# Chunk attention and two feed-forward layers on one Trainium2 core: the weights' preparation moved and split, and the last first product of a pair placed inside the first second product

## The chip, the core and the metric

One core of one Trainium2 chip runs one program. The time is device microseconds (us) of an execution; three executions of the kernel before took 1644.35 to 1645.06 us, median 1645.0. A profiled execution gives the rows below; their times count from the start of its span.

## The reference

```
scores = scale * q_c @ k_c^T            # chunks of 64 rows, 8 batches, 8 heads, 576 rows, 64 columns
attn   = exp(scores - max) / (sum + 1e-9)
x      = attn @ v_c                     # as 4608 tokens x 512
h = x @ w_in;  g = s * relu(h)**2 + b;        y   = g @ w_out     # 512 -> 2048 -> 512
h = y @ w_in2; g = h * sigmoid(1.702 * h);    out = g @ w_out2    # 512 -> 2048 -> 512
```

All is float32; the weights come as 64-bit floats that the kernel turns into float32 itself.

## The kernel before

**Numbers.** Every float32 operand of a large product is kept as two tiles, hi (rounded by ScalarE) and lo (VectorE's difference), and a product is three matmuls: lo by hi, hi by hi, hi by lo. A matmul has 128 rows of weights and 512 columns.

**Blocks.** The 4608 tokens are nine blocks of 512. Seven blocks of the first layer and one of the second are computed plainly: `gemm_in` (L554, 12 matmuls into one of two banks h) for each of 16 slices of the inner dimension, relu and square on ScalarE (L566, L567), hi and lo (L102, L103), and `gemm_out` (L629, 12 matmuls into four banks acc). A bank h is free again when its relu has read it.

**Pairs.** The other ten passes are taken as five pairs of blocks, by a scheme with seven products instead of eight, M1 to M7, on halves and their sums and differences. `PAIRS` lists them as layer and first block: (1, 1), (0, 7), (1, 3), (1, 5), (1, 7), layer 0 being the first. In each, eight steps i make the seven first products (`first`, L735): M1, M6, M7 and M4 add into one bank x of step i, M5 and M3 into a bank d, M2 has a bank b. `quarter` (L754 to L761) turns the banks into the four quarters of g: 11 from b, 12 from d, 22 from x after M7, 21 from x after M4. Then the seven second products follow (`second`, L834), each over the same eight i and for two halves z of its output; the first of them is M1. The banks of the second products for z = 0 and z = 1 are those that held x of steps 6 and 7, tags acc2 and acc3.

**Weights.** The first layer's weights are decoded at the start and stay as hi and lo. Beside the blocks run sixteen pieces of work for the pairs, one for each i of eight and each of w_in and w_out:
- `decode_second` loads two tiles of the second layer's weights (512 KB each), decodes them (L124 to L130 on ScalarE, VectorE and GpSimd), stores them in DRAM (`w2_dram`, by GpSimd's queue), makes four sums of their quarters on GpSimd (`add_quarters`, L221 to L224), rounds them on ScalarE (L209, 128x1024), subtracts (L211), and stores hi and lo.
- `sums` does the same with the first layer's weights, from the kept hi and lo (L240), with two roundings (L247) and four stores.
- `copies` copies three quarters of kept hi and lo to DRAM (256 KB each, L263).

When the first layer's plain blocks end, `second_weights` brings the 32 decoded tiles back (L228, 256 KB each) and splits them again (L150, L151).

**Order.** Each call has a time on a plan (`at`, `steps_at`); 32 units are one plain block. The calls are emitted in the order of these times, and a scheduler with a model of the engines then sets the order on each engine. Each engine takes its instructions strictly in that order. `behind` adds an order between two instructions of an engine. Loads and stores go through SP's queue in order, but for GpSimd's and a few of ScalarE's. Three buffers hold what is loaded for decoding (wst), ten hold temporary tiles (tmp), four hold v and the sums (vs).

Of the kernel before, what the change touches and what calls it, by code (L numbers as in the profile page):

```python
# [6 lines left out]
F32 = mybir.dt.float32  # L7
# [28 lines left out]

PLACE = {"M1": 0, "M2": 1, "M4": 2, "M5": 3, "M6": 4, "M7": 5, "M3": 6}
BANK = {"M1": "x", "M6": "x", "M7": "x", "M4": "x", "M5": "d", "M3": "d", "M2": "b"}  # L40
PAIRS = ((1, 1), (0, 7), (1, 3), (1, 5), (1, 7))
OUT_ORDER = ("M1", "M5", "M6", "M2", "M7", "M3", "M4")
# [3 lines left out]
def chunk_attention_two_ffn(ctx, tc, q, k, v, w1_in, w1_out, s, b, w2_in, w2_out, out):  # L46
# [145 lines left out]
    def decode_second(kind, i):  # L192
        tiles = i, i + KF // 2
        sts, ms = [], []
        for t in tiles:
            sts.append(staged())
            load_f64[kind](w2_in if kind == "wi" else w2_out, t, sts[-1])
            yield
        for t, st in zip(tiles, sts):
            m, c = tmp("wm"), tmp("wc")  # L200
            for _ in decode(st, m, c):
                pass
            nc.gpsimd.dma_start(out=w2_dram[kind][t], in_=m)
            ms.append(m.rearrange("p (t c) -> p t c", c=2 * P))
            yield
        s, hi = (st.rearrange("p f z -> p (f z)").bitcast(F32).rearrange("p (t c) -> p t c", c=2 * P) for st in sts)
        add_quarters(kind, s, ms)
        yield
        nc.scalar.activation(out=hi.bitcast(F32R), in_=s, func=AF.Copy)  # L209
        yield  # L210
        nc.vector.tensor_tensor(out=s.bitcast(F32R), in0=s, in1=hi, op=ALU.subtract)  # L211
        for part, src in enumerate((hi, s)):
            nc.sync.dma_start(out=sums_to(1, kind, i)[:, 3:7, part].rearrange("p m k c -> p m (k c)"), in_=src)

    def add_quarters(kind, s, tiles):

        one, two = tiles
        a11, a22 = one[:, 0, :], two[:, 1, :]
        a12, a21 = (one[:, 1, :], two[:, 0, :]) if kind == "wi" else (two[:, 0, :], one[:, 1, :])
        s1, s2, s3, s4 = (s[:, t, :] for t in range(4))  # L220
        nc.gpsimd.tensor_tensor(out=s1, in0=a21, in1=a22, op=ALU.add)  # L221
        nc.gpsimd.tensor_tensor(out=s3, in0=a11, in1=a21, op=ALU.subtract)
        nc.gpsimd.tensor_tensor(out=s2, in0=s1, in1=a11, op=ALU.subtract)
        nc.gpsimd.tensor_tensor(out=s4, in0=a12, in1=s2, op=ALU.subtract)  # L224

    def second_weights(kind, i):
        m = tmp("wm")
        nc.sync.dma_start(out=m, in_=w2_dram[kind][i])  # L228
        W[1, kind, i] = resident(1, kind, i, m)

    def sums_to(f, kind, i):
# [2 lines left out]
    def sums(kind, i):  # L234

        q = []
        for t in (i, i + KF // 2):
            hi, lo = (kept_parts[0, kind, t][:, a, :] for a in range(2))
            q.append(apool.tile([P, NB_MAX], F32, tag="vs", name="vs", bufs=HP))
            nc.vector.tensor_tensor(out=q[-1], in0=hi, in1=lo, op=ALU.add)  # L240
        yield
        q = [t.rearrange("p (t c) -> p t c", c=2 * P) for t in q]
        s = staged().rearrange("p f z -> p (f z)").bitcast(F32).rearrange("p (t c) -> p t c", c=2 * P)
        add_quarters(kind, s, q)
        yield
        for n, hi in enumerate(q):
            nc.scalar.activation(out=hi.bitcast(F32R), in_=s[:, 2 * n:2 * n + 2, :], func=AF.Copy)  # L247
        yield
        to = sums_to(0, kind, i)
        for n, hi in enumerate(q):  # L250
            part = s[:, 2 * n:2 * n + 2, :]
            nc.vector.tensor_tensor(out=part.bitcast(F32R), in0=part, in1=hi, op=ALU.subtract)
            for a, src in enumerate((hi, part)):
                nc.sync.dma_start(
                    out=to[:, 3 + 2 * n:5 + 2 * n, a].rearrange("p m k c -> p m (k c)"), in_=src
                )

    def copies(f, kind, i):

# [401 lines left out]
    class Halves:  # L661
# [63 lines left out]
        def first(self, i, m):  # L725
            key = i, BANK[m]
            start = key not in self.ps
            if start:
                self.bank(key, BANK[m], f"acc{i % KD}")
            w = self.wi[i][PLACE[m]]  # L730
            for k in range(HK):
                xh, xl = self.x[m, k]
                hi, lo = w[:, k, 0, :], w[:, k, 1, :]
                for a, (l_, r_) in enumerate(((lo, xh), (hi, xh), (hi, xl))):
                    nc.tensor.matmul(  # L735
                        out=self.ps[key], lhsT=l_, rhs=r_,
                        start=start and k == 0 and a == 0, stop=k == HK - 1 and a == 2,
                        skip_group_check=not start,
                    )

        def keep(self, key, name):
            self.kept[key[0], name] = t = tmp("kept")
# [25 lines left out]
        def plan_first(self):  # L768
            self.wi = {}

            def load(i):
                self.w = {}
                self.load_wi(i)
                self.wi[i] = self.w
            for i in range(HF):
                t = self.base + 3.5 * i
                at(t - 9, load, i)
                at(t, self.rooms_g, i)

                for n, m in ((0, "M1"), (0.5, "M5"), (1.5, "M6"), (2, "M2"), (2.5, "M3"), (3, "M7"), (4.5, "M4")):  # L780
                    at(t + n, self.first, i, m)
                at(t + 0.6, self.keep, (i, "x"), "M1")
                at(t + 1.1, self.keep, (i, "d"), "M5")
                at(t + 2.1, self.keep, (i, "x"), "M16")
                at(t + 2.6, self.quarter, i, "11")
                at(t + 3.1, self.quarter, i, "12")
                at(t + 3.6, self.quarter, i, "22")
                at(t + 5.1, self.quarter, i, "21")
# [33 lines left out]

        def second(self, n, i, zs=(0, 1)):
            m = OUT_ORDER[n]
            hi, lo = self.op[n, i]
            w = self.wo[n, i // 2]
            for z in zs:
                key = "out", z, BANK[m]
                start = m in ("M1", "M5", "M2")
                if start and i == 0:  # L830
                    self.bank(key, BANK[m], f"acc{HK + z}")
                wh, wl = (w[:, i % 2, z, part, :] for part in range(2))
                for a, (l_, r_) in enumerate(((wl, hi), (wh, hi), (wh, lo))):
                    nc.tensor.matmul(  # L834
                        out=self.ps[key], lhsT=l_, rhs=r_,
                        start=start and i == 0 and a == 0, stop=i == HF - 1 and a == 2,
                        skip_group_check=not start,
                    )

        def keep_out(self, z, bank, name):  # L840
            self.kept[z, name] = t = tmp("kept")
# [27 lines left out]
        def plan_second(self):  # L869
            self.wo = {}  # L870
            base = self.base + 3.5 * HF
            for n, m in enumerate(OUT_ORDER):
                for r in range(HF // 2):
                    at(base + 4 * n + r - 9, self.load_wo, n, r)
                for i in range(HF):
                    t = base + 4 * n + 0.5 * i
                    at(t - 3, self.operand, n, i)
                    if not (self.last and m == "M4"):
                        at(t, self.second, n, i)
                done = base + 4 * n + 4.1  # L880
                if self.last and m == "M4":
                    for z in range(2):
                        for i in range(HF):
                            at(base + 4 * n + 2 * z + 0.25 * i, self.second, n, i, (z,))
                        at(base + 4 * n + 2 * z + 2.1, self.result, "21", z)
                    continue
                for z in range(2):
                    if m in ("M1", "M5", "M6"):
                        at(done, self.keep_out, z, BANK[m], {"M6": "M16"}.get(m, m))
                    else:  # L890
                        at(done, self.result, {"M2": "11", "M7": "22", "M3": "12", "M4": "21"}[m], z)
# [67 lines left out]
        plan_attention(j)  # L959
    plan_y(0)  # L960
    for n, (i, kind) in enumerate((i, kind) for i in range(KF // 2) for kind in ("wi", "wo")):
        t = 56 + 9.3 * n
        steps_at([(t + d, 1) for d in (0, 1, 2.5, 4, 6, 8.5, 9.7)], lambda kind=kind, i=i: decode_second(kind, i))
        steps_at([(t + d, 1) for d in (2.2, 2.5, 5, 6.2)], lambda kind=kind, i=i: sums(kind, i))
        at(t + 3, copies, 0, kind, i)
    for i in range(KF):
        for n, kind in enumerate(("wi", "wo")):
            t = NS * (SINGLE - 1) + 2 * i + 1 + 3 * n
            at(t, second_weights, kind, i)
            if i >= KF // 2:  # L970
                at(t + 3, copies, 1, kind, i - KF // 2)
    def first_product(*a):
        G[a] = gemm_in(*a)

# [40 lines left out]
```

## Time and profile before

| | |
|---|---|
| three executions | 1644.35 to 1645.06 us, median 1645.0 |
| the profiled execution | 1644.05 us |
| its span, first to last instruction | 1642.3 us, mean granted TensorE clock 0.989 |
| busy: PE, DVE, ACT, POOL | 1584.4, 1125.5, 823.4, 250.7 us |

PE is TensorE, PEld its weight loads, DVE VectorE, ACT ScalarE, POOL GpSimd, SP SyncE (SPq its queue of transfers). PE is busy for 96% of the span, so what is left to gain is nearly all in the 58 us in which it is not, and in the stretches at the lower clock.

### The profile page before, as it was taken

What the parts mean: (1) busy time and instruction counts of PE and PEld (TensorE: products, weight loads), DVE (VectorE), ACT (ScalarE), POOL (GpSimd) and SP (SyncE); (2) the same over time, 40 slices, a digit from 0 to 9 for tenths busy, and PEclk for the clock granted to TensorE, in tenths of its full rate; (3) what the DMA queues carried; (4) which work ended last, traced back from release to release, by engine and by line L of the source; (5) the groups of instructions that cost most, each with busy time, mean ns of one, the idle gap of its engine ahead of it and who ended that gap; (6) DMA issues with size and microseconds to landing.
All of it is one profiled execution on the core that took longest, in us unless ns stands there. A gap on an engine that the chain in (4) does not pass through costs nothing.

```text
span 1642.3 us, 24873 instructions
## 1 busy us (share of the span) xinstructions
PE 1584.4 (96%) x8840; PEld 1295.1 (79%) x8840; DVE 1125.5 (69%) x1836; ACT 823.4 (50%) x1427; POOL 250.7 (15%) x286
## 2 busy tenths in 40 slices
PE   6889999999999999999999999999999999999998
PEld 4768887778888888777888788888887888788876
DVE  5667667768776676766745696369368946984685
ACT  3766424445544545545334564776345535543552
POOL 1344214234333334200000000000001000100000
PEclk8899999999999999999999999999999999999999
DMA  9747667666665666899606777786668686777764
GB/s 232 224 159 205 201 171 220 169 178 174 187 170 158 171 193 164 243 278 289 203 27 187 235 224 192 213 274 205 196 193 265 179 225 210 249 192 214 218 194 76
DMA packets 392396, 326.74 MB, mean 199 GB/s; under 512 B 256592, under 2 KB 330320, under 8 KB 392272
## 3 DMA queue, kind: packets, MB, share of 16 engines
q1 hardware_dynamic: 382096, 301.81, 65.0%
q0 software_dynamic: 5760, 18.88, 3.4%
q10 hardware_dynamic: 4416, 4.46, 0.8%
q8 instruction: 70, 1.15, 0.3%
q14 instruction: 54, 0.44, 0.1%
HBM read 232.78 MB, written 92.27 MB: 198 GB/s over the span
## 4 chain that ended last, share of the span: by engine, by line
PE 78%; DVE 7%; DMA 5%; ACT 3%; SPq 2%; issue 2%; POOL 2%; DVEq 0%; POOLq 0%; ACTq 0%
PE acc L629 15%; PE h L554 14%; PE x L735 13%; PE x L834 13%; PE d L834 7%; PE d L735 7%; PE b L735 3%; PE b L834 3%; DMA wm<-w_wi 2%; DVE pt L320 1%; PE xT L330 1%; PE sc L351 1%; SPq L452 1%; SPq L294 1%; DVE gl L103 1%
## 5 line engine op out<-in xcount | busy, mean ns | idle before, releaser
L554 PE MATMUL h<-xh,wi 128*128 128x512 f32 x1024 | 326.1, 400 | 19.1 <-ACT r L566 9.5
L629 PE MATMUL acc<-gh,wo 128*128 128x512 f32 x896 | 277.1, 393 | 2.7 <-ACT gh L102 2.7
L554 PEld LDWEIGHTS h<-xh,wi 128*128 128x128 f32 x1024 | 193.0, 192 | 62.6 <-ACT r L566 11.5
L554 PE MATMUL h<-xl,wi 128*128 128x512 f32 x512 | 202.2, 396 | 0.0
L629 PEld LDWEIGHTS acc<-gh,wo 128*128 128x128 f32 x896 | 166.3, 188 | 38.7 <-ACT gh L102 3.6
L629 PE MATMUL acc<-gl,wo 128*128 128x512 f32 x448 | 172.7, 392 | 2.0 <-DVE gl L103 1.9
L811 ACT ACTIVATE op<-wo 128x512 fp32r<-128x512 f32 x160 | 99.7, 631 | 98.1 <-PE x L834 35.9
L834 PE MATMUL x<-op,wi 128*128 128x512 f32 x540 | 130.7, 389 | 0.0
L735 PE MATMUL x<-xh,wi 128*128 128x512 f32 x400 | 124.3, 391 | 3.1 <-DVE wo L754 3.1
L812 DVE TENSOR_TENSOR op<-wo,op 128x512 fp32r<-128x512 f32 x160 | 107.2, 683 | 17.4 <-ACT op L811 15.9
L834 PEld LDWEIGHTS x<-op,wi 128*128 128x128 f32 x540 | 101.4, 188 | 21.1
L554 PEld LDWEIGHTS h<-xl,wi 128*128 128x128 f32 x512 | 98.3, 192 | 21.1
L659 DVE TENSOR_TENSOR wo<-wo 128x512 f32<-128x512 f32 x160 | 107.4, 686 | 4.5 <-ACT wo L757 3.7
L761 DVE TENSOR_TENSOR wo<-wo,r 128x512 f32<-128x512 f32 x96 | 66.0, 691 | 63.8 <-ACT r L760 63.4
L128 POOL TENSOR_TENSOR wm<-wm,wc 128x512 int32<-128x512 int32 x52 | 73.4, 1414 | 216.0 <-DVE wm L127 111.9
L674 POOL DMA_DIRECT2D xr<-y x32 | 17.6, 549 | 564.5 <-DVE op L812 278.8
L629 PEld LDWEIGHTS acc<-gl,wo 128*128 128x128 f32 x448 | 83.9, 188 | 21.6 <-DVE gl L103 4.0
L320 DVE STREAM_TRANSPOSE pt<-p 32x256 f32<-32x256 f32 x224 | 97.7, 436 | 3.9
L760 ACT ACTIVATE r<-wo 128x512 f32<-128x512 f32 x96 | 60.7, 632 | 75.8 <-DVE wo L754 75.1
L811 ACT ACTIVATE gh<-wo 128x512 fp32r<-128x512 f32 x120 | 74.7, 631 | 47.4 <-PE x L834 13.6
L812 DVE TENSOR_TENSOR gl<-wo,gh 128x512 fp32r<-128x512 f32 x120 | 81.4, 687 | 18.5 <-ACT gh L811 14.3
L735 PEld LDWEIGHTS x<-xh,wi 128*128 128x128 f32 x400 | 74.7, 188 | 20.5 <-DVE wo L754 5.2
(162 smaller groups left out, 3028.6 us busy)
## 6 DMA issues: line engine op xcount, KB each, us to landing
wi<-wo_sums SPq DMA_DIRECT2D x140, 512.0 KB, 4.2
wi<-wi_sums SPq DMA_DIRECT2D x120, 512.0 KB, 4.0
wst<-in_moe_w_out SPq DMA_DIRECT2D x32, 512.0 KB, 4.2
wst<-in_moe_w_in SPq DMA_DIRECT2D x24, 512.0 KB, 4.5
wi_sums<-wi SPq DMA_DIRECT2D x48, 256.0 KB, 4.0
wo_sums<-wo SPq DMA_DIRECT2D x48, 256.0 KB, 4.1
wi<-wi_sums SPq DMA_DIRECT2D x40, 256.0 KB, 3.6
y<-ost SPq DMA_DIRECT2D x36, 256.0 KB, 3.7
```

The source lines that it names most:

```text
L128: nc.gpsimd.tensor_tensor(out=t, in0=t, in1=c.bitcast(I32), op=ALU.add)
L320: nc.vector.transpose(out=pt[r.start + ek * BK:r.start + (ek + 1) * BK, :, eq * BK:(eq + 1) * BK], in_=p[r.start + eq * BK:r.start + (eq + ...
L554: nc.tensor.matmul(out=ps, lhsT=w_[:, kk, :], rhs=x_, start=kk == 0 and a == 0, stop=kk == KD - 1 and a == 2,)
L629: nc.tensor.matmul(out=acc[m], lhsT=l_, rhs=r_, start=i == 0 and a == 0, stop=i == KF - 1 and a == 2)
L659: nc.vector.tensor_tensor(out=to, in0=one, in1=two, op=ALU.subtract)
L674: nc.gpsimd.dma_start(out=t, in_=(y_dram if self.f else x_dram)[self.j + c][:, k + a * HK, :])
L735: nc.tensor.matmul(out=self.ps[key], lhsT=l_, rhs=r_, start=start and k == 0 and a == 0, stop=k == HK - 1 and a == 2, skip_group_check=not ...
L760: nc.scalar.activation(out=r, in_=h, func=AF.Sigmoid, scale=1.702)
L761: nc.vector.tensor_tensor(out=g, in0=h, in1=r, op=ALU.mult)
L811: nc.scalar.activation(out=hi, in_=src, func=AF.Copy)
L812: nc.vector.tensor_tensor(out=lo, in0=src, in1=hi.bitcast(F32), op=ALU.subtract)
L834: nc.tensor.matmul(out=self.ps[key], lhsT=l_, rhs=r_, start=start and i == 0 and a == 0, stop=i == HF - 1 and a == 2, skip_group_check=not ...
```

## The change

- The sixteen pieces start 6 units later, and within a piece the rounding of the decoded weights' sums and what follows comes 1 unit later; so does the rounding in `sums`.
- `sums` makes its four sums in place, in the two tiles vs that held the operands; the buffer wst is then taken only for the rounded halves. `PLACE` gives the products another order in DRAM (M1, M2, M4, M6, M7, M3, M5), which suits the tiles as they now lie.
- `second_weights` is split: the load three units before its old time, the splitting at the old time. The copies of the second weights get times of their own, after the last plain block of the first layer by the plan.
- In each pair M4 of the last step is planned at 4.2 instead of 4.5, the first second product goes z by z for six of its eight i, and its matmuls from i = 3 on are ordered behind that M4.

```diff
-PLACE = {"M1": 0, "M2": 1, "M4": 2, "M5": 3, "M6": 4, "M7": 5, "M3": 6}
+PLACE = {"M1": 0, "M2": 1, "M4": 2, "M6": 3, "M7": 4, "M3": 5, "M5": 6}
...
-        add_quarters(kind, s, ms)
+        add_quarters(kind, ms, [s[:, t, :] for t in (3, 0, 1, 2)])
...
-    def add_quarters(kind, s, tiles):
+    def add_quarters(kind, tiles, to=None):
...
-        s1, s2, s3, s4 = (s[:, t, :] for t in range(4))
+        s1, s2, s3, s4 = to or (a22, a11, a21, a12)
...
         nc.sync.dma_start(out=m, in_=w2_dram[kind][i])
+        yield
         W[1, kind, i] = resident(1, kind, i, m)
...
-        s = staged().rearrange("p f z -> p (f z)").bitcast(F32).rearrange("p (t c) -> p t c", c=2 * P)
-        add_quarters(kind, s, q)
+        add_quarters(kind, q)
         yield
-        for n, hi in enumerate(q):
-            nc.scalar.activation(out=hi.bitcast(F32R), in_=s[:, 2 * n:2 * n + 2, :], func=AF.Copy)
+        his = staged().rearrange("p f z -> p (f z)").bitcast(F32).rearrange("p (t c) -> p t c", c=2 * P)
+        his = [his[:, 2 * n:2 * n + 2, :] for n in range(2)]
+        for src, hi in zip(q, his):
+            nc.scalar.activation(out=hi.bitcast(F32R), in_=src, func=AF.Copy)
...
+            if m == "M4" and i == HF - 1:
+                marks["last first product", self.f, self.j] = latest(mybir.EngineType.PE)
...
-                for n, m in ((0, "M1"), (0.5, "M5"), (1.5, "M6"), (2, "M2"), (2.5, "M3"), (3, "M7"), (4.5, "M4")):
+                for n, m in ((0, "M1"), (0.5, "M5"), (1.5, "M6"), (2, "M2"), (2.5, "M3"), (3, "M7"), (4.2 if i == HF - 1 else 4.5, "M4")):
...
+            old = len(nc.cur_bb.bb.instructions)
...
+            if n == 0 and i == 3:
+                behind(old, mybir.EngineType.PE, ("last first product", self.f, self.j))
...
-                    if not (self.last and m == "M4"):
+                    if n == 0 and i < 6:
+                        for z in range(2):
+                            at(base + 6 / 4 * z + 0.25 * i, self.second, n, i, (z,))
+                    elif not (self.last and m == "M4"):
                         at(t, self.second, n, i)
...
-        t = 56 + 9.3 * n
-        steps_at([(t + d, 1) for d in (0, 1, 2.5, 4, 6, 8.5, 9.7)], lambda kind=kind, i=i: decode_second(kind, i))
-        steps_at([(t + d, 1) for d in (2.2, 2.5, 5, 6.2)], lambda kind=kind, i=i: sums(kind, i))
+        t = 62 + 9.3 * n
+        steps_at([(t + d, 1) for d in (0, 1, 2.5, 4, 6, 9.5, 10.7)], lambda kind=kind, i=i: decode_second(kind, i))
+        steps_at([(t + d, 1) for d in (2.2, 2.5, 6, 7.2)], lambda kind=kind, i=i: sums(kind, i))
...
-            at(t, second_weights, kind, i)
+            steps_at(((t - 3, 1), (t, 1)), lambda kind=kind, i=i: second_weights(kind, i))
             if i >= KF // 2:
-                at(t + 3, copies, 1, kind, i - KF // 2)
+                at(NS * SINGLE + 2.5 * (i - KF // 2) + 2 + n, copies, 1, kind, i - KF // 2)
```

In the listings that follow, a row is line, operation, written tile, read tiles, shape and count.

PE, at the end of the first products of the first pair. x_9405 is the bank x of step 7 (its last four rows here are M4), x_9499 the bank of the first second product for z = 0, x_9503 (after: x_9552) that for z = 1. Before:

```order
L834 MATMUL x_9499<-gh_9449,wi_9309 128x512 x2
L834 MATMUL x_9499<-gl_9450,wi_9309 128x512
L834 MATMUL x_9499<-op_9465,wi_9309 128x512 x3
L834 MATMUL x_9499<-op_9476,wi_9335 128x512 x3
L834 MATMUL x_9499<-op_9491,wi_9335 128x512 x3
L834 MATMUL x_9499<-op_9507,wi_9356 128x512 x3
L735 MATMUL x_9405<-xh_8477,wi_9214 128x512 x2
L735 MATMUL x_9405<-xl_8478,wi_9214 128x512
L735 MATMUL x_9405<-xo_8741,wi_9214 128x512 x2
L735 MATMUL x_9405<-xo_8742,wi_9214 128x512
L834 MATMUL x_9503<-gh_9423,wi_9289 128x512 x2
L834 MATMUL x_9503<-gl_9424,wi_9289 128x512
```

The same place after:

```order
L837 MATMUL x_9499<-gl_9438,wi_9289 128x512
L837 MATMUL x_9499<-gh_9449,wi_9309 128x512 x2
L837 MATMUL x_9499<-gl_9450,wi_9309 128x512
L735 MATMUL x_9405<-xh_8471,wi_9214 128x512 x2
L735 MATMUL x_9405<-xl_8472,wi_9214 128x512
L735 MATMUL x_9405<-xo_8741,wi_9214 128x512 x2
L735 MATMUL x_9405<-xo_8742,wi_9214 128x512
L837 MATMUL x_9499<-op_9465,wi_9309 128x512 x3
L837 MATMUL x_9499<-op_9476,wi_9335 128x512 x3
L837 MATMUL x_9499<-op_9491,wi_9335 128x512 x3
L837 MATMUL x_9499<-op_9503,wi_9356 128x512 x3
L837 MATMUL x_9552<-gh_9423,wi_9289 128x512 x2
```

M4 of step 7 has moved up past twelve matmuls of z = 0, which now stand between it and the first matmul of z = 1. All five pairs have this.

ACT, in the first piece whose rounding L209 stands close before a relu (L566) of block 2. wst_2790 and wst_2799 (after: wst_2677 and wst_2698) are the two buffers of the decoded weights, h the banks of `gemm_in`. Before:

```order
L247 ACTIVATE vs_2821<-wst_2833 128x512
L247 ACTIVATE vs_2823<-wst_2833 128x512
L102 ACTIVATE xh_2921<-xT_2879 128x512
L209 ACTIVATE wst_2799<-wst_2790 128x1024
L364 ACTIVATE p_2943<-p_2943 128x512
L566 ACTIVATE r_2982<-h_2967 128x512
L566 ACTIVATE r_3024<-h_3009 128x512
```

The corresponding place after, one piece earlier in the row of pieces (the first w_in piece instead of the first w_out piece):

```order
L249 ACTIVATE wst_2804<-vs_2731 128x512
L102 ACTIVATE xh_2885<-xT_2845 128x512
L249 ACTIVATE wst_2804<-vs_2729 128x512
L209 ACTIVATE wst_2698<-wst_2677 128x1024
L364 ACTIVATE p_2907<-p_2907 128x512
L566 ACTIVATE r_2944<-h_2929 128x512
L567 ACTIVATE r_2944<-r_2944 128x512
L566 ACTIVATE r_2981<-h_2966 128x512
```

One whole piece, which before stood here already done, has moved behind this block's start; the two roundings of `sums` (L247, now L249) and L209 still stand ahead of the relu.

SP, around the load of w2_wo1 (the second w_out tile brought back) in block 6. Before:

```order
L228 DMA wm_7038<-w2_wi2_102 128x512
L254 DMA wo_sums0_148<-wst_7093 128x2x256
L294 DMA ks_7251<-in_k 32x14x32
L339 DMA x7_150<-xo_7043 128x512
L294 DMA ks_7251<-in_k 32x14x32 x2
L294 DMA qs_7250<-in_q 32x2x32 x4
L294 DMA ks_7251<-in_k 32x2x32 x4
L304 DMA vs_7370<-in_v 64x7x64 x2
L304 DMA vs_7370<-in_v 64x64
L228 DMA wm_7098<-w2_wo1_117 128x512
L228 DMA wm_7131<-w2_wi3_103 128x512
L228 DMA wm_7156<-w2_wo2_118 128x512
```

After:

```order
L228 DMA wm_6866<-w2_wi2_102 128x512
L263 DMA wi_sums10_140<-wi_6840 128x2x256 x2
L294 DMA qs_7216<-in_q 32x14x32 x4
L228 DMA wm_6907<-w2_wo1_117 128x512
L294 DMA ks_7217<-in_k 32x14x32 x4
L650 DMA y5_157<-ost_6924 128x512
L294 DMA qs_7216<-in_q 32x2x32
L650 DMA y5_157<-ost_6930 128x512
L650 DMA y5_157<-ost_6927 128x512
L294 DMA qs_7216<-in_q 32x2x32
L534 DMA yst_6936<-y0_152 128x512
L228 DMA wm_6941<-w2_wi3_103 128x512
```

The load of w2_wo1 now stands before the loads of k and before this block's stores of y, where it stood behind them and behind v; the copies (L263) still stand among the loads.

## Rows read from the trace of the kernel before

**Rows 1.** The page: span, and busy us by engine.

```profile
span 1642.3 us, 24873 instructions
PE 1584.4 (96%) x8840; PEld 1295.1 (79%) x8840; DVE 1125.5 (69%) x1836; ACT 823.4 (50%) x1427; POOL 250.7 (15%) x286
```

**Rows 2.** PE's waits, whole span: waiter, releaser: us in total, times, longest.

```profile
PE h L554 <- ACT r L566: 9.5, 4, 4.3
...
PE x L834 <- DVE wo L761: 5.8, 4, 1.5
...
PE acc L629 <- ACT gh L102: 2.7, 1, 2.7
...
PE x L834 <- ACT wo L756: 0.7, 1, 0.7
```

**Rows 3.** Stretches: us, busy of PE, PEld, DVE, ACT, POOL, clock, DMA, GB/s.

```profile
240.00:280.00 40.00, 38.01 (x264) 30.10 (x263) 29.00 (x44) 16.24 (x28) 15.98 (x18) 0.96 0.80 223
280.00:320.00 40.00, 35.67 (x201) 28.48 (x200) 35.16 (x53) 18.22 (x31) 12.64 (x14) 0.96 0.69 178
...
720.00:760.00 40.00, 37.17 (x212) 29.02 (x211) 24.61 (x42) 23.56 (x41) 0.00 (x0) 1.00 1.03 300
```

**Rows 4.** Timeline, end of a pair's first products: start, us, instruction, idle before.

```profile
1245.72 0.69 DVE L754 TENSOR_TENSOR wo<-x,kept 128x512 f32<-128x512 f32 x1 [0.23 <-PE x L735]
...
1247.56 2.88 PE L834 MATMUL x<-op,wi 128*128 128x512 f32 x12
...
1251.90 0.60 ACT L760 ACTIVATE r<-x 128x512 f32<-128x512 f32 x1 [1.41 <-PE x L735]
1252.53 0.69 DVE L761 TENSOR_TENSOR wo<-x,r 128x512 f32<-128x512 f32 x1 [1.32 <-ACT r L760]
...
1253.27 0.73 PE L834 MATMUL x<-gh,wi 128*128 128x512 f32 x2 [1.47 <-DVE wo L761]
```

**Rows 5.** Timeline of all engines, block 2, around PE's longest wait there.

```profile
286.66 1.05 POOL L224 TENSOR_TENSOR wst<-wm,wst 128x256 f32<-128x256 f32 x1
...
287.74 1.06 ACT L209 ACTIVATE wst<-wst 128x1024 fp32r<-128x1024 f32 x1 [3.94 <-POOL wst L224]
...
290.76 1.06 ACT L566 ACTIVATE r<-h 128x512 f32<-128x512 f32 x2
...
291.39 1.22 PE L554 MATMUL h<-xh,wi 128*128 128x512 f32 x2 [4.33 <-ACT r L566]
```

**Rows 6.** POOL's timeline, the start of the run that ends in rows 5.

```profile
273.75 1.52 POOL L128 TENSOR_TENSOR wm<-wm,wc 128x512 int32<-128x512 int32 x1 [10.90 <-DVE wm L127]
```

**Rows 7.** Groups of instructions by line: busy, mean ns of one.

```profile
L812 DVE TENSOR_TENSOR gl<-wo,gh 128x512 fp32r<-128x512 f32 x120 | 81.4, 687 | 18.5 <-ACT gh L811 14.3 <-PE x L834 2.2 <-PE b L834 0.7
...
L128 POOL TENSOR_TENSOR wm<-wm,wc 128x512 int32<-128x512 int32 x52 | 73.4, 1414 | 216.0 <-DVE wm L127 111.9 <-ACT r L567 22.2 <-ACT gh L102 22.0
L103 DVE TENSOR_TENSOR gl<-r,gh 128x512 fp32r<-128x512 f32 x80 | 69.5, 873 | 8.2 <-ACT gh L102 7.9
```

**Rows 8.** Timeline, block 6: a second weight is loaded, split, and waited for.

```profile
683.99 0.53 SPq L228 DMA_DIRECT2D wm<-w_wo  x1
...
687.04 0.63 ACT L150 ACTIVATE wo<-wm 128x512 fp32r<-128x512 f32 x1 [4.87 <-DMA wm<-w_wo]
687.58 0.61 ACT L102 ACTIVATE gh<-r 128x512 fp32r<-128x512 f32 x1
...
688.25 0.73 PE L629 MATMUL acc<-gh,wo 128*128 128x512 f32 x2 [2.67 <-ACT gh L102]
```

**Rows 9.** PE's timeline, 720 to 800 us: two of its waits.

```profile
732.19 0.73 PE L554 MATMUL h<-xh,wi 128*128 128x512 f32 x2 [2.26 <-ACT r L566]
...
770.96 0.73 PE L554 MATMUL h<-xh,wi 128*128 128x512 f32 x2 [1.47 <-DVE r L570]
```

**Rows 10.** Transfers: count, KB each, median us from issue to landing.

```profile
wm<-w_wo SPq DMA_DIRECT2D x16, 256.0 KB, 4.5
```

**Rows 11.** DVE's timeline, 276 to 285 us.

```profile
278.97 4.23 DVE L103 TENSOR_TENSOR gl<-r,gh 128x512 fp32r<-128x512 f32 x1
```

More of the change, by code (lines that the diff above doesn't have):

```diff
@@ L242, in sums @@
         q = [t.rearrange("p (t c) -> p t c", c=2 * P) for t in q]
-        s = staged().rearrange("p f z -> p (f z)").bitcast(F32).rearrange("p (t c) -> p t c", c=2 * P)
-        add_quarters(kind, s, q)
+        add_quarters(kind, q)
         yield
-        for n, hi in enumerate(q):
-            nc.scalar.activation(out=hi.bitcast(F32R), in_=s[:, 2 * n:2 * n + 2, :], func=AF.Copy)
+        his = staged().rearrange("p f z -> p (f z)").bitcast(F32).rearrange("p (t c) -> p t c", c=2 * P)
+        his = [his[:, 2 * n:2 * n + 2, :] for n in range(2)]
+        for src, hi in zip(q, his):
+            nc.scalar.activation(out=hi.bitcast(F32R), in_=src, func=AF.Copy)
         yield
[L249 to L256, printed above, removed]
+        sums = sums_to(0, kind, i)[:, 3:7]
+        for n, (src, hi) in enumerate(zip(q, his)):
+            nc.vector.tensor_tensor(out=src.bitcast(F32R), in0=src, in1=hi, op=ALU.subtract)
+            to = sums[:, n::2] if kind == "wi" else sums[:, 2 * n:2 * n + 2]
+            for a, part in enumerate((hi, src)):
+                nc.sync.dma_start(out=to[:, :, a].rearrange("p m k c -> p m (k c)"), in_=part)
     def copies(f, kind, i):
```

## The prediction

> **What bounds the kernel now.** I read the busy times first: PE is busy 1584.4 of 1642.3 us [rows 1], so the time can fall only where PE stands still (58 us) or runs at the lower clock. Second, PE's waits with their releasers over the whole span. Those that the change can touch are five [rows 2]: 9.5 us for relu L566 on ScalarE in four waits, 5.8 us in four for the quarter L761, 0.7 us in one for L756 (the same place in the pair of layer 0), 2.7 us in one for the rounding L102. A good part of the other idle time lies at the start, before the first pieces, where the order on PE is the same before and after. Third, the table of stretches: in 240 to 320 us PE is busy 73.68 of 80 us and the granted clock is 0.96 in both stretches of 40 us; in 720 to 760 us PE is busy 37.17 of 40 us and the transfers use all that the 16 DMA engines have, share 1.03 [rows 3]. Last, the timeline at each of these waits [rows 4, 5, 8, 9], to see who is late and why. So there are three places with something to gain: the end of each pair's first products, block 2 with the first pieces, and block 6 with the second weights.
>
> **Part 1, the pairs.** Before, M4 of step 7 is the last thing that PE issues ahead of the first matmul for z = 1, which writes the very bank that M4 filled. ScalarE (L760, 0.60 us) and VectorE (L761, 0.69 us) must read that bank first, so PE stands for 1.47 us [rows 4]. After, twelve matmuls of z = 0 stand between M4 and z = 1. They are those that took 2.88 us as one row [rows 4], which covers the 1.47 us twice over. Does M4 get a wait in exchange? It adds to bank x of step 7 after the quarter L754 has read it. L754 ended at 1245.72 + 0.69 = 1246.41 us, and M4 can now start where the twelve began, at 1247.56 us: 1.15 us to spare. The operands of the twelve matmuls were there earlier than they are now needed. On ScalarE and VectorE L760 and L761 come right behind what they followed before, so they start 2.88 us earlier too. All five pairs have the same order here: the gain is 5.8 + 0.7 = 6.5 us [rows 2]. If the cover failed in part, it would be worth less, but hardly below 5. The new times of the second product's z halves alter nothing else: the matmuls are the same. The new order of loading (M5 last) costs nothing as long as each step's weights come two steps ahead, as they do in the order.
>
> **Part 2, the pieces in blocks 2 to 5.** The pieces' work is the same in count and size: the sums in place are the same four operations of VectorE's size on GpSimd, with the same roundings and stores. What changes is what stands in front of whom. Before, L209 stood on ScalarE just ahead of a relu while GpSimd was still at the sums: it waited 3.94 us for L224, ScalarE's queue stood with it, and PE waited 4.33 us for the relu behind it [rows 5]. GpSimd's run for this piece began at 273.75 us [rows 6] and ended at 286.66 + 1.05 = 287.71 us. After, a piece stands here whose L209 still comes ahead of the relu, but whose decoding started earlier relative to the block. By hand I follow it: two L128 of 1.41 us [rows 7], eight sums of about 1.05 us [rows 5], 11.2 us in all, from about 271.5 (estimate, 2 us ahead of rows 6 because its decoding isn't behind the first two transposes) to 282.7 us, or to 284.8 us with gaps like those of before (13.96 us in rows 5 and 6 for the like work). L209 takes 1.06 us, and 2 us later the relu can run, at 284 to 288 us, where PE needs it at 291.39 - 4.33 = 287.06 us. So the wait falls from 4.33 us to 0 to 1: I count 3.3 us. The clock is the second half. A mean of 0.96 over 40 us is 40 x 0.04 / 0.5 = 3.2 us at half of full speed, so at the lower of its two levels, and such a stretch loses 1.6 us of matmul work; there is one in each of the two windows [rows 3], and the one in 280 to 320 us came behind the long wait. With that wait gone I count 1.6 us back; the other stays, since the wait at the start of the block (part of the 9.5 us) stays as well. The two remaining waits of this kind before 400 us are 9.5 - 4.33 - 2.26 [rows 9] = 2.9 us; I leave them. Sum of the part: -4.9 us, between -8 (the other slow stretch and a wait go too) and +2 (the run of before is merely moved to another block). The nearest row is the 4.33 us wait itself, so I take the value near it.
>
> **Part 3, the second weights in blocks 6 and 7.** Before, the load and the splitting L150 of a tile were one step. The load was issued when the plan called for the tile, behind what was already in SP's queue. L150 then waited on ScalarE 4.87 us for a transfer issued at 683.99 us, the rounding L102 stood behind it, and PE waited 2.67 us [rows 8]; like transfers land 4.5 us after issue in the median [rows 10]. In the new order the loads stand further up: that of w2_wo1 behind 6 transfers instead of 16 after that of w2_wi2, so it leaves the queue earlier by some ten issues. At 0.53 us for an issue [rows 8] that is about 5 us, as long as L150 waited. So I take the 2.67 us as gone. The waits of 2.26 and 1.47 us [rows 9] lie in the stretch where the DMA share is 1.03 [rows 3]; an earlier place in the queue doesn't make that fuller traffic quicker, so of these 3.73 us I count a third, 1.3 us. The copies barely move in the emitted order, whatever their plan times say, so they take nothing out of the stretch. Sum: -4.0 us, between -7 (all three and a little more) and +2.
>
> **Part 4, what the change adds.** Each second weight holds its temporary tile longer, by the time between load and L150; there are ten such tiles, and the decoding, relu and squares take tiles from the same pool. On SP a load that must wait for a free tile holds back the loads of q, k and v behind it. And the pieces end 6 units later, which pushes the last ones into block 6. No row of before shows either; the nearest are the waits of 1.47 to 2.67 us [rows 8, 9], of which I allow one: +2 us, between 0 and 6. A few copies of the first weights are now issued about 20 us earlier, when nothing waits for the queue; I count 0, plus or minus 0.5.
>
> **The sum.** 1644.05 - 6.5 - 4.9 - 4.0 + 2.0 = 1630.65 us in terms of the profiled execution. The median of the runs is 0.95 us above it, so 1631.6 us. The terms' ends reach from -21 to +5; together they seldom all fall on one side.
>
> **A rule that speaks against it.** DVE's L103 takes 873 ns in the mean beside the decoding, where L812, the same operation on the same shape in the pairs without GpSimd, takes 687 [rows 7]; one L103 took 4.23 us in the middle of GpSimd's run [rows 11]. The Trainium skill, page "SBUF — State Buffer", section "Who interferes with whom", states that a VectorE instruction with two SBUF inputs contends with a GpSimd instruction that reads SBUF, that whoever comes first holds the shared ports for its whole instruction, and that the other is blocked until then. By that rule, the trace agrees in direction: the row of 4.23 us can be a wait behind several operations of GpSimd in turn. The sum above holds no term of it, as the number of GpSimd's operations stays; it is the last rival.
>
> **The rivals.**
> - *Only the pairs pay* (chance 0.18). The waits of parts 2 and 3 are passed on to the neighbouring block, as they hang on a model's order that missed them before too. For it: the waits of 9.5 us come at four quite different places [rows 2]. Against: the load stands ten places earlier, which no model's error undoes. 1645.0 - 6.5 = 1638.5 us, from 1636 to 1641.
> - *The tiles and the queue hold it up* (chance 0.12). The early loads keep tiles from the pool, in the stretch in which the transfers already use all of the engines; the full 6 us of part 4 come, and parts 2 and 3 give nothing or a little back. 1645.0 - 6.5 + 6 = 1644.5 us, from 1641.7 to 1648.3. Against: ten tiles, and the loads are only some ten issues earlier.
> - *GpSimd holds VectorE* (chance 0.07), the slower side. The sums in place run in one row with the decoding, without the gaps in which VectorE got in, and each piece costs VectorE a wait such as that of [rows 11], 4.23 - 0.69 = 3.5 us [rows 7], that the relu's chain passes on to PE. It decides from the third piece that costs PE all of it: 6.5 us of gain in the pairs plus 3.3 us bound need 9.8 / 3.5 = 2.8 of the sixteen, if parts 2 and 3 give nothing. With four pieces 1645.0 - 6.5 + 14 = 1652.5 us. Against: VectorE is busy 29.00 and 35.16 of 40 us in the pieces' stretches [rows 3] and can make up some of it, and L103 is late now without PE waiting for it.
>
> **How the numbers follow.** The forecast, 1631.6 us, has the chance 0.63, with its own range 1624 to 1637. What a measurement can tell from no change is 0.2%, 3.3 us. Faster than 1641.7 us are the forecast and the first rival, 0.81; within 0.2% the second, 0.12; slower than 1648.3 us the third, 0.07. The range of 8 in 10 reaches over the first rival to 1641 us and below to 1623.5 us, where parts 2 and 3 pay in full.
>
> **What would show it.** In the profile after: the waits of PE for L761 and L756 ahead of z = 1 are gone (0 of 6.5 us), and the wait of M4 for L754 doesn't grow. The wait for L566 falls from 9.5 us to below 5; the clock in 280 to 320 us is 1.00. PE's idle time in 680 to 800 us falls by 3 to 5 us, and L150 waits under 2 us for its transfer. L103's mean stays below 0.9 us. The forecast is wrong if PE's idle time in 240 to 680 us grows, if SP waits for tiles ahead of the second weights, or if the pairs' waits move to M4.

## The result: slower by 0.55%, and where the profile has the time

The changed kernel took 1654.92 us (median of 4, 1652.34 to 1656.37) against 1645.03 us for the kernel before: ratio 1.0055, 95% interval 1.0037 to 1.0073. The forecast was 1631.6 us, faster. Below, a ratio is always that of a kernel to the kernel before on the same chip, and 0.001 of it is 1.645 us.

The page of the kernel after, its head and busy times (us, share of the span, instructions), against [rows 1]:

```profile
span 1654.2 us, 24871 instructions
...
PE 1590.6 (96%) x8840; PEld 1297.7 (78%) x8840; DVE 1141.2 (69%) x1836; ACT 823.3 (50%) x1427; POOL 255.5 (15%) x286
```

The span is 11.9 us longer: PE works 6.2 us longer and stands 5.7 us longer. Over the whole span the mean granted clock is the same, 0.989: the trace of before has more of the lower clock in the first 240 us (0.94 against 0.97), the trace of after has more of it later. VectorE, with as many instructions, is busy 15.7 us longer. PE's waits over the whole span, as in [rows 2]:

```profile
PE acc L629 <- DVE gl L103: 9.1, 10, 2.1
...
PE h L554 <- ACT r L566: 5.0, 4, 2.3
PE acc L629 <- DVE ost L640: 4.8, 3, 1.7
PE x L735 <- DVE wo L756: 3.5, 5, 0.8
PE acc L629 <- ACT ost L644: 2.0, 1, 2.0
```

Two lines of before, to compare with them:

```profile
PE x L735 <- DVE wo L754: 3.1, 4, 0.8
...
PE acc L629 <- DVE gl L103: 1.9, 2, 1.4
```

The waits ahead of z = 1 are gone, the first products' wait for L756 (L754 before) hardly grew, and the wait for relu L566 fell from 9.5 to 5.0 us, much as forecast. New are 6.8 us for L640 and L644, the evacuations: at the end of a block they read the four banks acc that the next block's `gemm_out` wants. The wait for L103 grew from 1.9 to 9.1 us. PE's idle time in 240 to 680 us grew from 8.7 to 20.1 us, which the forecast had named as a sign of being wrong; in 680 to 800 us it stayed at 7.7 us instead of falling by 3 to 5. Counting the columns of the matmuls in PE's order, I compared when each kernel has done the same work. After lags by +2.5 us where before is at 447 us, +10.5 at 494, +10.4 at 588, +22.5 at 682, +19.4 at 834 and +11.9 at the end. So the pairs give 7.5 us back, and blocks 3 to 6 lose 20.

Stretches of the kernel after (columns as in [rows 3]):

```profile
280.00:320.00 40.00, 36.74 (x266) 29.19 (x264) 37.48 (x55) 18.49 (x31) 16.41 (x21) 1.00 0.75 205
320.00:360.00 40.00, 37.56 (x214) 29.86 (x211) 23.24 (x39) 18.91 (x34) 14.29 (x17) 0.96 0.55 155
...
480.00:520.00 40.00, 36.87 (x216) 29.45 (x212) 31.52 (x51) 19.64 (x32) 16.56 (x20) 0.91 0.69 194
680.00:720.00 40.00, 36.05 (x254) 28.94 (x253) 33.32 (x52) 23.56 (x40) 12.69 (x13) 0.91 0.91 265
720.00:760.00 40.00, 36.83 (x220) 29.14 (x220) 25.78 (x50) 20.32 (x34) 5.33 (x7) 0.96 0.97 263
```

The two slow stretches of 3.2 us in 240 to 320 us [rows 3] are gone, but two as long stand in 320 to 360 and 720 to 760 us. New are two of 40 x 0.09 / 0.5 = 7.2 us, each worth 3.6 us of matmul work, where two evacuations are late. The first of the two places, on VectorE, ScalarE and PE:

```profile
469.38 0.69 DVE L241 TENSOR_TENSOR vs<-wi 128x512 f32<-128x512 f32 x1 [3.21 <-DMA wo_sums<-vs]
...
474.17 3.60 DVE L320 STREAM_TRANSPOSE pt<-p 32x256 f32<-32x256 f32 x8
...
477.86 0.78 ACT L644 ACTIVATE ost<-acc,shift,sb 128x512 f32<-128x512 f32 x1 [4.99 <-DVE pt L320]
...
481.18 0.69 DVE L130 SCALAR_TENSOR_TENSOR wm<-wst,wm 128x512 int32<-128x512 int32 x1 [1.17 <-POOL wm L128]
...
482.12 0.81 DVE L640 TENSOR_SCALAR ost<-acc,sb,shift 128x512 f32<-128x512 f32 x1
...
482.99 0.73 PE L629 MATMUL acc<-gh,wo 128*128 128x512 f32 x2 [1.69 <-DVE ost L640]
...
483.87 1.05 PE L629 MATMUL acc<-gh,wo 128*128 128x512 f32 x2
...
486.79 1.22 PE L629 MATMUL acc<-gh,wo 128*128 128x512 f32 x2 [1.44 <-DVE ost L640]
```

Read from the end: PE waits for L640; L640 stands on VectorE behind the attention's transposes L320 and three decoding steps, one of which (L130) waits 1.17 us for GpSimd; L320 is late because L241, the first operation of the next piece's `sums`, stood on VectorE 3.21 us for a store of the sums before it to leave its tile vs. L644 waits for L320 too, presumably because its tile ost takes the buffer that L320 still read.

### The profile page after: what moved, and what is told of

Same layout as the page of the kernel before. It is cut to its first block, busy times and chain, and to the rows that moved or that the text cites. A ratio compares the mean times of both kernels' runs of the same rounds, so it can differ in the third digit from the quotient of the medians.

```text
span 1654.2 us, 24871 instructions
## 1 busy us (share of the span) xinstructions
PE 1590.6 (96%) x8840; PEld 1297.7 (78%) x8840; DVE 1141.2 (69%) x1836; ACT 823.3 (50%) x1427; POOL 255.5 (15%) x286
## 4 chain that ended last, share of the span: by engine, by line
PE 72%; DVE 10%; DMA 6%; issue 3%; POOL 3%; ACT 3%; SPq 3%; DVEq 0%; POOLq 0%; ACTq 0%
PE x L735 13%; PE x L837 13%; PE acc L629 12%; PE h L554 11%; PE d L837 7%; PE d L735 6%; PE b L837 3%; PE b L735 3%; DVE pt L320 2%; SPq L294 2%; DMA wm<-w_wi 1%; DVE gl L103 1%; PE sc L351 1%; PE xT L330 1%; DMA wo_sums<-wst 1%
## 5 line engine op out<-in xcount | busy, mean ns | idle before, releaser
L735 PE MATMUL x<-xh,wi 128*128 128x512 f32 x400 | 124.1, 390 | 3.5 <-DVE wo L756 3.5
L629 PEld LDWEIGHTS acc<-gl,wo 128*128 128x128 f32 x448 | 84.9, 190 | 32.4 <-DVE gl L103 14.7
L320 DVE STREAM_TRANSPOSE pt<-p 32x256 f32<-32x256 f32 x224 | 97.6, 436 | 3.9
L735 PEld LDWEIGHTS x<-xh,wi 128*128 128x128 f32 x400 | 74.7, 188 | 20.8 <-DVE wo L756 5.6
```

What stands on the lines that cost most here:

```text
L320: nc.vector.transpose(out=pt[r.start + ek * BK:r.start + (ek + 1) * BK, :, eq * BK:(eq + 1) * BK], in_=p[r.start + eq * BK:r.start + (eq + ...
L629: nc.tensor.matmul(out=acc[m], lhsT=l_, rhs=r_, start=i == 0 and a == 0, stop=i == KF - 1 and a == 2)
L735: nc.tensor.matmul(out=self.ps[key], lhsT=l_, rhs=r_, start=start and k == 0 and a == 0, stop=k == HK - 1 and a == 2, skip_group_check=not ...
```

## The experiments

All are timed against the kernel before. The first set: the pairs' edit alone, and the changed kernel with one of its other parts undone.

**pairs_only**: the kernel before with only this (and the `behind` with its mark):

```diff
+(4.2 if i == HF - 1 else 4.5, "M4")
+if n == 0 and i < 6: (z by z)
```

> The kernel before with the pairs' edit alone (M4 of the last step at 4.2, the first second product z by z, its matmuls from i = 3 on behind M4). Both theories say the same: five waits of 1.3 to 1.8 us go, so about 8 us less than before, 1637 us (1636 to 1639), with the order before 800 us as it was. If it is not below 1641 us, the gain read from the changed kernel's stretch after 800 us belongs to something else.

1634.02 us, ratio 0.9955 (0.9943 to 0.9967): 7.4 us gained, with the order before 800 us as it was.

**no_times**: `t = 62 + 9.3 * n` back to 56, the roundings' times too.

> The changed kernel with the pieces' times of before (56 instead of 62, the late roundings one unit earlier). Theory 1 (the new times put a piece's decoding at the ends of blocks, where it stands ahead of the evacuation of the banks acc on VectorE and ScalarE): the waits of L629 for L640 and L644 (6.8 us) and the stretches at the lower clock that follow (about 5 us) go, 1636 to 1642 us. Theory 2 (sums in place hold the tiles vs longer): they stay, 1652 to 1656 us. Theory 3 (early second weights): stays too.

1644.64 us, 1.0014 (1.0002 to 1.0025).

**no_sums**: `add_quarters(kind, q)` back to sums in a buffer wst, the old `PLACE`.

> The changed kernel without the sums in place (sums go to a buffer wst as before, old order of the products in DRAM). Theory 1: the block ends are still hit, 1650 to 1656 us. Theory 2 (the tiles vs are held until the sums are stored, so the loads of v and the next sums wait, and GpSimd runs against VectorE): 1640 to 1646 us.

1638.73 us, 0.9976 (0.9965 to 0.9987).

**no_second**: `second_weights` in one step, `copies` at `t + 3`.

> The changed kernel with the second weights loaded and split in one step at their old time, and the copies at their old times. Theory 1: only the stretch from 680 us on can change, by at most the waits there, 1649 to 1658 us. Theory 3 (the early loads hold temporary tiles that the evacuations and the decoding need): 1638 to 1646 us, with the waits at 686 and 689 us gone.

1651.63 us, 1.0057 (1.0044 to 1.0069). So the second weights' part changes nothing beside the other two (theory 3 falls), and two parts each seem to cost: undoing the sums in place gives 13 us back, undoing the times 7. Neither theory alone accounts for it. The next set puts one part each beside the pairs, and tries to take VectorE's wait away.

**pairs_sums**: pairs_only plus the sums in place and `PLACE`.

> The kernel before with the pairs' edit and the sums in place, nothing else. If the sums in place cost by themselves (their tiles vs go out only behind the rounding that waits for a buffer wst, the next sums' first operation L240 then stands on VectorE): 1641 to 1646 us, about 8 to 11 above the pairs alone. If they cost only together with the new times (theory 1): 1633 to 1637 us.

1647.93 us, 1.0025 (1.0014 to 1.0036): 0.0070 above the pairs, 11.5 us. The sums in place cost by themselves.

**pairs_times**: pairs_only plus `t = 62 + 9.3 * n` and the later roundings.

> The kernel before with the pairs' edit and the pieces' new times, nothing else. Theory 1 (phase of the pieces against the ends of blocks): 1636 to 1641 us, with the waits of L629 for the evacuations of rows like those of the run without the sums in place. If the times cost nothing by themselves: 1632 to 1635 us.

1636.93 us, 0.9951 (0.9939 to 0.9963): the times alone neither cost nor gain. The wait of 4.3 us in block 2 is gone, and the clock in 240 to 320 us is 1.00, but PE now waits 1.83 and 1.71 us at two block ends and 2.83 us here:

```profile
592.00 0.50 PE L629 MATMUL acc<-gl,wo 128*128 128x512 f32 x1 [2.83 <-DVE gl L103]
```

**pairs_second**: pairs_only plus the second weights' part.

> The kernel before with the pairs' edit and the second weights' part, nothing else. By the prediction's part 3 it should be 4 us faster than the pairs alone, 1630 us; by the comparison of the changed kernel with and without this part it is within 2 us of the pairs alone, 1632 to 1637 us, since its waits are only moved within 680 to 800 us.

1633.16 us, 0.9930 (0.9918 to 0.9942): 0.0025 below the pairs, 4.1 us, which is part 3 of the forecast and not what I had come to expect. It is the fastest by ratio of all that ran. The wait of 2.67 us [rows 8] is 0.55 us here.

With this set the pairs' edit has been timed with every combination of the three other parts; a difference of two ratios is uncertain by some 3 us. The sums in place cost 11.5 us alone, 17.4 beside the times (no_second against pairs_times), 13.8 beside the second weights' part (no_times against pairs_second) and 13.0 beside both (the changed kernel against no_sums). The times gain 0.7 us alone, but cost 5.3 beside the sums (no_second against pairs_sums), 7.6 beside the second weights' part (no_sums against pairs_second) and 6.7 beside both.

**late_operands**: in the changed kernel,

```diff
-(2.2, 2.5, 6, 7.2)
+(3.7, 4, 6, 7.2)
```

> The changed kernel with the first two steps of each piece's sums (the operands' additions L241 on VectorE and the four sums on GpSimd) 1.5 units later, about 4 us, so that the store of the sums before them has landed. If VectorE's wait for those stores (17.7 us in 15 waits between 240 and 680 us) is what makes the evacuations late: it falls below 6 us, the waits of L629 at the block ends go, 1640 to 1646 us. If the phase of the decoding alone decides: no gain, 1649 to 1656 us.

1657.25 us, 1.0076 (1.0064 to 1.0088). The edit missed its aim: VectorE's waits for the stores rose to 22.0 us instead of falling, perhaps since the plan's later time also moved what follows. It tells nothing against the theory, and shows that a time on the plan isn't a place in the order.

So what differs with the sums in place? pairs_only, VectorE's and SP's timeline at the end of block 4:

```profile
558.82 1.52 DVE L240 TENSOR_TENSOR vs<-wi 128x512 f32<-128x512 f32 x2 [0.17 <-DMA wo_sums<-vs]
...
562.61 3.60 DVE L320 STREAM_TRANSPOSE pt<-p 32x256 f32<-32x256 f32 x8
...
572.11 1.52 DVE L640 TENSOR_SCALAR ost<-acc,sb,shift 128x512 f32<-128x512 f32 x2
...
554.49 1.85 SPq L294 DMA_DIRECT2D ks<-in_k  x4
556.52 1.21 SPq L254 DMA_DIRECT2D wo_sums<-vs  x2
557.82 1.00 SPq L254 DMA_DIRECT2D wo_sums<-wst  x2
```

pairs_sums, the same instructions (lines one less):

```profile
563.06 0.69 DVE L240 TENSOR_TENSOR vs<-wi 128x512 f32<-128x512 f32 x1 [2.91 <-DMA wo_sums<-vs]
...
567.82 3.60 DVE L319 STREAM_TRANSPOSE pt<-p 32x256 f32<-32x256 f32 x8
...
576.68 0.80 DVE L639 TENSOR_SCALAR ost<-acc,sb,shift 128x512 f32<-128x512 f32 x1
...
577.53 1.22 PE L628 MATMUL acc<-gh,wo 128*128 128x512 f32 x2 [1.90 <-DVE ost L639]
...
557.68 1.85 SPq L293 DMA_DIRECT2D ks<-in_k  x4
...
560.50 0.41 SPq L255 DMA_DIRECT2D wo_sums<-vs  x1
561.01 0.44 SPq L255 DMA_DIRECT2D wo_sums<-wst  x1
561.54 0.45 SPq L255 DMA_DIRECT2D wo_sums<-vs  x1
```

The amounts are the same, but the tile vs has changed its part. Before, it took the rounded half, which is ready first and was stored first: both stores of vs start within 556.52 to 557.73. In place, it holds the difference, ready only after the subtraction and stored among the others: the last at 561.54. It is free about 4 us later, and L240, which wants it, stands on VectorE 2.91 us in front of the attention. Most of the 4 us is not the tile's new part, though: the four loads of k that stand ahead of the stores in SP's queue are 3.2 us later as well (557.68 against 554.49), so about 1 us of it is left for the order of the stores here. The next set tests this, and a mixed timing of the pieces.

**vs_late**: pairs_only, sums in wst as before, only the stores' order changed:

```diff
+tc.add_manual_dep(store_of_hi_in_vs, last_store_of_wst, IN_ORDER)
```

> The pairs alone, with the sums in a buffer wst as before, but the stores of the tiles vs (the rounded halves) made to follow the stores of wst, which wait for VectorE's subtraction. Theory 4: the sums in place cost since a tile vs then holds the late part (the difference) instead of the early one (the rounded half), so that it is stored some 3 us later and the next piece's L240 stands on VectorE ahead of the attention at a block's end. If so, this order alone brings back a good part of the 11.5 us: 1639 to 1646 us, VectorE's waits for the stores of vs above 15 us. If the cost is in the buffer wst or in GpSimd's operations: 1633 to 1636 us, as the pairs alone.

1643.9 us, 0.9997 (0.9988 to 1.0007): 0.0042 above the pairs, 6.9 us from an order of stores alone. VectorE's waits for these stores between 240 and 680 us, in pairs_only

```profile
DVE vs L240 <- DMA wi_sums<-vs: 8.1, 4, 3.3
DVE vs L240 <- DMA wo_sums<-vs: 1.9, 4, 0.8
```

and in vs_late (us in total, times, longest):

```profile
DVE vs L240 <- DMA wi_sums<-vs: 16.8, 6, 5.7
DVE vs L240 <- DMA wo_sums<-vs: 8.4, 6, 2.2
```

The places are others than in pairs_sums, though. The largest wait for an evacuation is at the end of block 2, and again L240 stands on VectorE ahead of it:

```profile
364.68 1.48 DVE L240 TENSOR_TENSOR vs<-wo 128x512 f32<-128x512 f32 x2 [5.68 <-DMA wi_sums<-vs]
...
379.28 0.73 PE L630 MATMUL acc<-gh,wo 128*128 128x512 f32 x2 [2.00 <-DVE ost L641]
```

**vs_soon**: pairs_sums with the stores of vs ahead of those of wst, the subtraction at 5.1 instead of 6.2.

> The pairs and the sums in place, with the stores of the tiles vs made to come before those of wst, and the subtraction one unit earlier on the plan. Theory 4: the tiles come free 1 to 2 us sooner, 1639 to 1645 us, VectorE's waits for the stores of vs below 12 us. If the cost is elsewhere: 1646 to 1650 us as with the sums in place.

1647.64 us, 1.0018 (1.0007 to 1.003), within the interval of pairs_sums. The waits for the stores fell only from 17.9 to 14.7 us, so the dose was small, and it took none of the cost back.

**drift**: pairs_second with `t = 62 + 9.3 * n - 1.2 * min(5, max(0, n - 1))`.

> The pairs and the second weights' part, with the pieces starting 6 units later at first and drawn together until they stand as before from the seventh on (62 + 9.3 n less 1.2 for each piece from the second, at most 6). The wait of 4.3 us in block 2 and the slow stretch behind it go as in the run with the new times alone, about 4 us, and the ends of the later blocks keep their phase: 1629 to 1632 us. If drawing the pieces together makes the three buffers wst late: 1633 to 1638 us.

1634.59 us, 0.9942 (0.9929 to 0.9954), no better than pairs_second. The wait of 4.3 us is gone and is given back later in waits of 1.7 to 2.0 us: the times trade waits.

Last, the order at the block ends. In pairs_sums ScalarE has this at the end of block 5; L643 is the evacuation:

```profile
677.18 1.15 ACT L248 ACTIVATE wst<-vs 128x512 fp32r<-128x512 f32 x2 [3.43 <-issue]
678.24 0.76 ACT L643 ACTIVATE ost<-acc,shift,sb 128x512 f32<-128x512 f32 x1
```

The rounding L248 now takes the buffer wst itself, where GpSimd's L221 did before, so it can stand 3.43 us on ScalarE in front of an evacuation. "issue" names no cause here; by the program it is the store of an earlier piece that reads the buffer, which the profile names at other waits. Waits of 240 to 680 us, in pairs_only and then in pairs_sums, where L221 waits for no such store:

```profile
POOL wst L221 <- DMA wi_sums<-wst: 53.3, 7, 9.4
POOL wst L221 <- DMA wo_sums<-wst: 51.2, 7, 9.2
```

```profile
ACT wst L248 <- DMA wo_sums<-wst: 21.9, 6, 5.4
ACT wst L248 <- DMA wi_sums<-wst: 15.6, 5, 4.9
```

**round_after**: pairs_sums plus

```diff
+behind(old, ACT, last evacuation on ScalarE)   # the rounding L248
```

> The pairs and the sums in place, with the rounding L249 of each piece's sums ordered behind the evacuation emitted last; in effect two roundings at the end of block 5 change places with L645 (PE's order is the same). Theory 5 (the second wait is that rounding, 3.4 us on ScalarE for a buffer wst ahead of the evacuation): the wait of L630 for L645 of 3 us at 679 us and the slow stretch behind it go, 4 to 5 us less than with the sums in place, 1642 to 1645 us. If the evacuation is late for another reason there: 1646 to 1650 us.

1648.15 us, 1.0028 (1.0017 to 1.0039), no gain. The wait of 2.96 us for L643 at 679 us did go. By the same count of columns as above, 4 us were won there and lost again at 701 us, where the next L102 stood behind the splitting L150 of a second weight, which waited for its load:

```profile
699.84 0.63 ACT L150 ACTIVATE wo<-wm 128x512 fp32r<-128x512 f32 x1 [5.01 <-DMA wm<-w_wo]
...
701.04 1.22 PE L630 MATMUL acc<-gh,wo 128*128 128x512 f32 x2 [4.78 <-ACT gh L102]
```

**both**: vs_soon plus that, plus

```diff
+behind(old, DVE, last evacuation on VectorE)   # the next sums' L240
```

> The pairs and the sums in place, with the tiles vs stored first, the rounding ordered behind ScalarE's last evacuation and the next sums' first operation on VectorE behind VectorE's last evacuation. If the two waits together are the cost: 1634 to 1640 us, near the pairs alone. If a third cause is left, or the order on the other engines decides: 1642 to 1648 us.

1632.3 us, 0.9934 (0.9921 to 0.9947): 0.0091 below pairs_sums, 15 us, and no slower than the pairs alone. With the sums in place as they are, the order of a few waiting instructions takes their whole cost away. VectorE's waits for the stores fell from 17.9 to 7.1 us, and PE waits for no evacuation in 240 to 800 us, against 4.9 us in pairs_sums. At the end of block 4 the sums' first operation (L241 here) stands behind both evacuations of VectorE (L647) and waits for nothing:

```profile
568.97 1.52 DVE L647 TENSOR_SCALAR ost<-acc,sb,shift 128x512 f32<-128x512 f32 x2
570.41 1.83 DVE L241 TENSOR_TENSOR vs<-wi 128x512 f32<-128x512 f32 x2
```

By the count of columns, pairs_sums falls behind pairs_only by 5.6 us at the end of block 4 and by 4.6 at that of block 5, of 13 us in the two profiles; at these two places *both* is 3.7 and 4.3 us quicker than pairs_sums. The new `PLACE` is in *both* too, so the order in DRAM is not the cost. Two runs are missing: L240's order without the rounding's, and the two orders without the sums in place. In pairs_only PE waits for no evacuation in 240 to 800 us, so they would have no such wait to remove there.

**after_fixed**: the changed kernel with three edits of *both*: the tiles vs stored first, the rounding and L240 behind the evacuations (the subtraction keeps its time).

> The changed kernel, all of its parts, with the tiles vs stored first and the sums' first operation on VectorE and the rounding on ScalarE ordered behind the evacuation emitted last. If these two waits are the cause in it too: the waits of L629 for the evacuations at 483 and 687 us go, 1636 to 1644 us, 8 to 16 less than the changed kernel. If the pieces' new times do harm of their own through the decoding at the block ends: 1645 to 1652 us.

1639.49 us, 0.9969 (0.9958 to 0.998): 0.0086 below the changed kernel, 14 us, and faster than before. PE no longer waits for an evacuation anywhere in 240 to 800 us; its largest waits there (the 5.4 us are for a relu at 694.60 us):

```profile
PE h L562 <- ACT r L574: 9.4, 4, 5.4
PE acc L637 <- DVE gl L103: 4.7, 7, 1.2
```

**both_second**: both plus the second weights' part.

> The run with both orders (no new times) and the second weights' part. If the parts add up: 4 us below the run without that part, 1628 to 1630 us. If they meet in 660 to 800 us, where both change ScalarE's and SP's order: 1631 to 1636 us.

1636.29 us, 0.9944 (0.9925 to 0.9963). The parts don't add up: the second weights' part gains 4 us beside the pairs, and nothing clear of noise beside the sums in place, here or in no_second.

## Why the prediction was wrong, step by step

**Part 1 was right.** -6.5 us forecast, -7.4 measured (pairs_only). In the kernel after, M4 (L735), the twelve matmuls and z = 1 run without a wait:

```profile
1264.79 0.62 PE L735 MATMUL x<-xh,wi 128*128 128x512 f32 x2
...
1266.15 2.88 PE L837 MATMUL x<-op,wi 128*128 128x512 f32 x12
1268.87 0.62 PE L837 MATMUL x<-gh,wi 128*128 128x512 f32 x2
```

**Part 2 failed, and with it the sum.** The step is "the pieces' work is the same in count and size: the sums in place are the same four operations". I costed the edit by its instructions and put it at nothing. It cost 11.5 us (pairs_sums against pairs_only), and 13.0 to 17.4 beside the other parts, by what waits where: L240 waits on VectorE for the tile vs to be stored; and the wait for a buffer wst, which GpSimd bore with time to spare, is now ScalarE's own. Both came to stand in front of evacuations at block ends, where PE then waits 1.4 to 3.0 us and stretches at the lower clock stand beside these waits. That it is the order is shown (both, after_fixed). Of the single causes, the order of the stores alone was shown to bring 6.9 us, at other places than the sums do (vs_late); storing the tiles first took nothing back by itself (vs_soon). How the cost splits between the two waits is open: with the rounding alone out of the way, what was won at one place was lost at the next second weight (round_after).

The other half of part 2, the new times, I had put at -4.9 us for the wait and clock in block 2. Both went as forecast, and alone the times are worth -0.7 us (pairs_times), inside the intervals: waits at later block ends took it back. Beside the other parts they cost 5 to 8 us; what they meet there was not followed and is open. I followed one block by hand and left the other four at nothing. (The hand count has a slip: 271.5 us and the 13.96 us of before make 285.5, not 284.8. GpSimd's run ended at 283.2 us.)

**Part 3 was right alone and wrong in company**: -4.0 us forecast, -4.1 beside the pairs (uncertain by some 3), 0 in the changed kernel. **Part 4's** +2 us stood for the tiles tmp. Those of vs, which the edit touched, were not among the costs at all.

**The rivals.** Of *GpSimd holds VectorE* the slower side was right, but its mechanism was not shown, and that its 1652.5 us lies near the measured time is luck. L103 did grow in the kernel after, against 873 ns in [rows 7]:

```profile
L103 DVE TENSOR_TENSOR gl<-r,gh 128x512 fp32r<-128x512 f32 x80 | 81.9, 1025 | 8.2 <-ACT gh L102 8.1
```

That is 80 x 0.152 = 12.2 us of VectorE's work. The direction is in line with the Trainium skill's rule on the shared port ("SBUF — State Buffer", section "Who interferes with whom"). But the time doesn't go with the mean: it is 884 ns in pairs_only and 948 in pairs_sums; vs_soon has 896 and is as slow as pairs_sums, *both* has 920 and is no slower than pairs_only, and vs_late loses 6.9 us with 894. It may feed the lateness; it isn't what decides.

*The tiles and the queue hold it up* isn't it either: without the early loads the changed kernel takes as long (no_second). *Only the pairs pay* fits the second weights' part as it came out in company, and left out that a part could cost.

## What to carry to other kernels

An edit that leaves every operation as it was can still change which half of a result a shared tile holds, and so when the tile comes free; ask of each buffer who releases it last, and on which engine the next taker waits. A wait is cheap on an engine with idle time (GpSimd here) and dear on one whose queue holds what frees PE's banks: order the waiting instructions behind the evacuations. And measure parts one by one, since three parts that cost or gain -4, -1 and +12 us alone came to +16 over the pairs together.

## Not expected of the hardware

In the kernel after, the granted clock is 0.91 over 480 to 520 us, so 7.2 us at the lower level. It fell between two waits of PE: behind the wait of 1.69 us two matmuls at 482.99 still took 0.73 us, two at 483.87 took 1.05, and the wait of 1.44 us came after that (1.22 us for two at 486.79). The wait of 2.83 us at 592 us in pairs_times was longer than either, had a matmul at full pace right behind it (0.50 us), and the granted clock of 560 to 600 us is 1.00. How long one wait is did not tell by itself whether the clock falls.
